# Output weights of six heads per layer by transfers of eight rows, in place of two or three heads by transfers of four

## Chip, cores and metric

The kernel runs on one core of one Trainium2 chip. The metric is the device time of one execution in microseconds (us), the median of several runs. Every microsecond in a profile counts from the start of the profiled execution's span.

## The reference

Two layers are computed, with the same weights and the same key and value cache in both. Each is a grouped-query attention block for decoding (two sequences, one new token each) followed by a gated feed-forward block, with residual additions.

```python
def _A_ref(x, k_cache, v_cache, wq, wo):          # x [2, 1, 512], caches [2, 8, 32768, 128]
    q = (x @ wq).reshape(B, Sq, Hq, Dh).transpose(0, 2, 1, 3)   # 32 query heads of 128
    k = jnp.repeat(k_cache, rep, axis=1)                         # 4 query heads per cached head
    v = jnp.repeat(v_cache, rep, axis=1)
    scores = jnp.einsum("bhqd,bhkd->bhqk", q, k) * (Dh ** -0.5)
    p = _softmax(scores, axis=-1)
    o = jnp.einsum("bhqk,bhkd->bhqd", p, v)
    return o.transpose(0, 2, 1, 3).reshape(B, Sq, Hq * Dh) @ wo

def _B_ref(x, w_gate, w_up, w_down):              # 512 -> 1792 -> 512
    h = _gelu(x @ w_gate) * (x @ w_up)
    return h @ w_down

x = x + _A_ref(_layernorm(x), ...)
x = x + _B_ref(_layernorm(x), ...)
x = x + _A_ref(_layernorm(x), ...)
x = x + _B_ref(_layernorm(x), ...)
```

All values are 32-bit floats. The caches alone are 537 MB, and each layer reads nearly all of them.

## The kernel before

The kernel keeps one large tile `mem` of 128 partitions by 109 units; a unit is 512 floats per partition. All weights and cache pieces pass through it. `stream` is a queue, written out in advance, of every transfer in the order in which its data are used. `pump` (L183) takes transfers from its head for as long as the next one fits into a hole of `mem`, and issues them on the SyncE queue (SP). `get` hands a landed piece to TensorE and `done` gives its units back and pumps again. So the depth of the queue in front of the DMA engines is set by how early units come free. Most cache pieces are 32 units (`CHUNK`), and three of them and 13 spare units fill `mem`. Pieces that are cut fine at the layer boundary have places written out by hand in `plan`.

Within a layer the loop runs over 16 pairs of cached head and sequence (`orders`; layer 1 goes backwards). For each pair, `scores` multiplies the query by the keys (L414), `softmax` follows, `values` multiplies by the values (L485), and `combine` leaves the four query heads' outputs in `oT`. After both sequences of a cached head, `project` multiplies `oT` by the head's slices of the output weights and adds into the PSUM bank `W`. The output weights come in groups of one or two cached heads (`WO_GROUPS`), queued between the two halves of a value transfer. The last cached head of a layer goes by `last_head` (L559). Then follow `residual` and `feedforward` (gate and up weights in four pieces for each of two halves, L638; down weights, L623 and L559).

For one cached head per layer, listed in `NARROW`, some of the query heads' weights don't lie on all 128 partitions. They are laid out on 16 (`NROW`) partitions, so that each row is eight times as long. In layer 0 this is head 6 with two of its four query heads, in layer 1 head 1 with three. Their transfer is issued as four transfers of four rows each:

```python
for i in range(4):
    nc.sync.dma_start(mem[i:NROW:4, c:c + cols], src[i])
```

Row r of such a transfer lies on partition i + 4r. `narrow` cuts `oT` into eight slices of 16 rows by matmuls with columns of the identity (L511), copies them to SBUF (L514), and multiplies each slice by its part of the weights (L519). The remaining query heads of that cached head come by an ordinary transfer of 128 partitions and are multiplied at L529. Narrow weights always take a whole `CHUNK` of 32 units.

Of the kernel before, what the change touches and what calls it, by code (L numbers as in the profile page):

```python
# [16 lines left out]
P = 128  # L17
NB = 2
HKV = 8
REP = 4  # L20
DM = 512
# [6 lines left out]
HALF = 2048  # L28
# [11 lines left out]
ORDER = [(g, b) for g in range(HKV) for b in range(NB)]  # L40
# [19 lines left out]
WO_GROUPS = [[(0, 1), (2, 3), (4, 5), (6,), (7,)], [(7,), (6,), (5, 4), (3, 2), (1,), (0,)]]  # L60


NARROW = {(0, HKV - 2): 2, (1, 1): 3}
NROW = 16
NSEL = P // NROW


def pieces(split):

    out, s = [], 0  # L70
    for n in split:
        out.append((s, n))
        s += n
    return out
# [61 lines left out]
def block_kernel(ctx: ExitStack, tc: tile.TileContext, x, consts, kt, vt, wq, wo, won, gu, wd, out):  # L136
    nc = tc.nc
# [12 lines left out]
    def take(key, n):  # L150
        if key in planned:
            o = planned[key]
            if not any(s <= o and o + n <= e for s, e in holes):
                return None
        elif n == CHUNK:
            spots = [o for o in range(0, UNITS - CHUNK + 1, CHUNK)
                     if any(s <= o and o + n <= e for s, e in holes)]
            if not spots:
                return None
            o = spots[0]  # L160
        else:
            fit = [(e - s, -s, e) for s, e in holes if e - s >= n]
            if not fit:
                return None
            size, s, e = min(fit)
            o = -s
        for i, (s, e) in enumerate(holes):
            if s <= o and o + n <= e:
                holes[i:i + 1] = [(x, y) for x, y in ((s, o), (o + n, e)) if y > x]
                return o  # L170
        return None

    def give(o, n):
        holes.append((o, o + n))
        holes.sort()
        i = 0
        while i + 1 < len(holes):
            if holes[i][1] == holes[i + 1][0]:
                holes[i:i + 2] = [(holes[i][0], holes[i + 1][1])]
            else:  # L180
                i += 1

    def pump():  # L183
        while stream:
            key, src, rows, cols = stream[0]
            n = CHUNK if rows == NROW else cols / UNIT if key in planned else -(-cols // UNIT)
            o = take(key, n)
            if o is None:
                return
            stream.popleft()  # L190
            c = int(o * UNIT)
            at[key] = (o, n), mem[:rows, c:c + cols]
            if rows == NROW:


                for i in range(4):
                    nc.sync.dma_start(mem[i:NROW:4, c:c + cols], src[i])
            else:
                nc.sync.dma_start(at[key][1], src)

    def flat_of(key):
        if key not in at:
            pump()
        return at[key][1]

    def get(key, a):
        return flat_of(key).rearrange("p (a c) -> p a c", a=int(a))

    def done(key, s=0, n=None):
# [10 lines left out]
    def flat(src, g, b, s, n):  # L220
        h, c = divmod(s, CHUNK)
        return src[b, g, h, :, c * UNIT:(c + n) * UNIT]

    def add(key, src, rows, cols):
        stream.append((key, src, rows, cols))

    def meets(l, n):

        return (l == 0 and n == len(ORDER) - 1), (l == 1 and n == 0)

    def wo_group(l, g):
        return next(t for t in WO_GROUPS[l] if g in t)

    for l in range(2):
        for i, (s, m) in enumerate(pieces(WQ_SPLIT[l])):
            add(("wq", l, i), wq[:, s * DM:(s + m) * DM], P, m * DM)
        for n, (g, b) in enumerate(orders[l]):
            second = meets(l, n)[1]
            vp = parts("v", l, (g, b))
            for s, m in parts("k", l, (g, b)):  # L240
                add(("k", l, g, b, s), flat(kt, g, b, s, m), P, m * UNIT)
            for s, m in [] if second else vp:
                if n % 2 == 1 and s == vp[1][0] and not meets(l, n)[0]:
                    group = wo_group(l, g)
                    o = g % 2 * HALF
                    if (l, g) in NARROW:
                        h = NARROW[l, g]
                        add(("won", l, g), won[l, :, :, :h * NSEL * DM], NROW, h * NSEL * DM)
                        add(("wo", l, g), wo[g // 2, :, o + h * DM:o + HALF], P, (REP - h) * DM)
                    elif len(group) == 2 and g == group[0]:  # L250
                        add(("wo", l, g), wo[g // 2], P, 2 * HALF)
                    elif len(group) == 1:
                        add(("wo", l, g), wo[g // 2, :, o:o + HALF], P, HALF)
                add(("v", l, g, b, s), flat(vt, g, b, s, m), P, m * UNIT)
            if meets(l, n)[0]:

                add(("wo", l, g), wo[g // 2, :, g % 2 * HALF:(g % 2 + 1) * HALF], P, HALF)
        for e in range(2):
            half_of = gu[e * P * FH:(e + 1) * P * FH].rearrange("(p c) -> p c", p=P)
            for j, (c, m) in enumerate(pieces(GU_SPLIT[l])):  # L260
                add(("gu", l, len(GU_SPLIT[l]) * e + j), half_of[:, c:c + m], P, m)
        for j, (o, m) in enumerate(pieces(WD_SPLIT[l])):
            add(("wd", l, j), wd[:, o * DM:(o + m) * DM], P, m * DM)
# [5 lines left out]
    def cut(n=1, shape=None):  # L269
# [12 lines left out]
    ident = cst[:, C_ID:C_ID + P]  # L282
# [22 lines left out]
    twice = {n: [cut(m, k) for _ in range(2)] for n, m, k in  # L305
             [("rstd", 1, None), ("ls", 2, None), ("xn", KC * NB, KC), ("oT", REP * NB, REP)]}
# [4 lines left out]
    def tiny(name):  # L311
        if name in once:
            return once[name]
        twice[name].reverse()
        return twice[name][1]
# [4 lines left out]
    W = ps.tile([P, 512], F32, name="W")  # L320
# [181 lines left out]
        diag = bass.AP(tensor=mt.tensor, offset=mt.offset, ap=[mt.ap[0], [1, REP], [P + REP, 4], [32, 4]])  # L502
        nc.vector.tensor_reduce(oT[:, :, b], diag, axis=AX.XY, op=OP.add)  # L503

    def narrow(l, g, oT, final):

        m = small()
        heads = NARROW[l, g]
        n = heads * NB
        for j in range(NSEL):  # L510
            nc.tensor.matmul(m[:NROW, n * j:n * j + n], ident[:, NROW * j:NROW * j + NROW],  # L511
                             oT[:, :heads, :].rearrange("p t b -> p (t b)"), start=True, stop=True)
        on = big()[:NROW, :NSEL * n]
        nc.vector.tensor_copy(on, m[:NROW, :NSEL * n])  # L514
        w = get(("won", l, g), NSEL * heads)
        for i in range(NSEL * heads):
            q = i % 4
            j, t = i % NSEL, i // NSEL
            nc.tensor.matmul(W[32 * q:32 * q + NB, :], on[:, n * j + NB * t:n * j + NB * t + NB], w[:, i, :],  # L519
                             start=False, stop=(final and q < heads and i + 4 >= NSEL * heads))  # L520
        done(("won", l, g))

    def project(l, g, oT, first, final):
        if (l, g) in NARROW:
            narrow(l, g, oT, final)
            h = NARROW[l, g]
            w = get(("wo", l, g), REP - h)
            for t in range(h, REP):
                nc.tensor.matmul(W[32 * t:32 * t + NB, :], oT[:, t, :], w[:, t - h, :], start=False, stop=final)  # L529
            done(("wo", l, g))  # L530
            return
        group = wo_group(l, g)
        key = "wo", l, group[0]
        w = get(key, REP * len(group))
        o = REP * (g - min(group))
        for t in range(REP):
            nc.tensor.matmul(W[32 * t:32 * t + NB, :], oT[:, t, :], w[:, o + t, :], start=first, stop=final)  # L537
        if g == group[-1]:
            done(key)

# [126 lines left out]
    for l in range(2):  # L667
        queries(l)
        stage(l, 0)
        for n, (g, b) in enumerate(orders[l]):  # L670
            if n % 2 == 0:
                oT = tiny("oT")
            p, linv = softmax(*scores(l, n, g, b))
            if meets(l, n)[0]:
                stash(g, b)
            stage(l, n + 1)
            values(l, n, g, b, p)
            combine(linv, oT, b, 128 if n == len(ORDER) - 1 else 0)
            if n == len(ORDER) - 1:
                last_head(l, g, oT)  # L680
            elif n % 2 == 1:
                project(l, g, oT, n == 1, n == len(ORDER) - 3)
            if n == len(ORDER) - 3:
                turn(xin)
        residual()
        feedforward(l)
        if l == 0:
            residual()
# [58 lines left out]
```

## Time and profile before

| | before |
|---|---|
| time, median of 3 runs | 2570.76 us (2570.63 to 2570.87) |
| span of the profiled execution | 2568.7 us |
| TensorE busy | 1374.8 us (54%) |
| VectorE, ScalarE, GpSimd busy | 143.6, 81.4, 2.4 us |
| moved by the SP queue | 1103.44 MB in 27136 packets |
| mean rate over the span | 430 GB/s |

The profile is of one execution; its span runs from the first to the last profiled instruction, and the measured time lies 2.1 us above it. The page lists busy time by engine, then the span in 40 slices, the DMA queues, the chain of work that ended last (each step followed back to what released it), the costliest groups of instructions, and the DMA issues. Queues are told by number: q1 is what SP issues, q8 carries instructions to the engines. A transfer of 128 partitions is spread over the 16 DMA engines, eight rows to each; the trace gives a packet's time and size but not its engine. In the window view a row has, after the engines' busy times, the granted TensorE clock, the mean busy share of the 16 DMA engines and the GB/s that they moved. In the view of transfers for a window, "under 512 B" counts packets by size, each class including the smaller ones.

### The profile page before, as it was taken

The page shows a single profiled execution, that of the slowest core. Times are in us where ns is not written, and L with a number is a line of the kernel's source. Part 1 is how long each engine was busy: PE and PEld are TensorE (multiplying, and loading weights), DVE is VectorE, ACT ScalarE, POOL GpSimd, SP SyncE. Part 2 cuts the span into 40 slices and gives each one's busy share as a digit, 9 for nine tenths or more (in the row PEclk, how much of TensorE's full clock was granted, in tenths as well). Part 3 has the DMA queues.
Part 4 walks back from the last instruction along what each step waited for, and adds up shares of the span by engine and source line. Part 5 has one row for each costly group of instructions (what it writes and reads, how often), then busy time and mean ns, then how long its engine had stood idle before and what let it go on. Part 6 is the DMA issues. An engine that isn't in the chain of part 4 may idle for free.

```text
span 2568.7 us, 20340 instructions
## 1 busy us (share of the span) xinstructions
PE 1374.8 (54%) x9526; PEld 369.8 (14%) x9526; DVE 143.6 (6%) x483; ACT 81.4 (3%) x188; POOL 2.4 (0%) x8
## 2 busy tenths in 40 slices
PE   3545555545544554564686554454555544554657
PEld 1111111111111111111121111111111111111112
DVE  0000000000000000000011000000000000000001
ACT  0000000000000000000000000000000000000000
POOL 0000000000000000000000000000000000000000
PEclk8777777777777777777798677677776777777779
DMA  9999999999999999999999999999999999999998
GB/s 425 429 434 434 428 437 431 432 433 434 429 438 428 435 433 431 434 431 432 424 410 438 429 433 434 430 433 435 431 434 432 431 435 431 433 433 430 431 432 371
DMA packets 27507, 1104.81 MB, mean 430 GB/s; under 512 B 3200, under 2 KB 3456, under 8 KB 6912
## 3 DMA queue, kind: packets, MB, share of 16 engines
q1 hardware_dynamic: 27136, 1103.44, 99.6%
q8 instruction: 74, 1.21, 0.2%
q10 hardware_dynamic: 288, 0.08, 0.0%
q14 instruction: 9, 0.07, 0.0%
HBM read 1103.45 MB, written 0.07 MB: 430 GB/s over the span
## 4 chain that ended last, share of the span: by engine, by line
DMA 69%; PE 22%; another core or an unknown queue 8%; DVE 1%; issue 0%; ACT 0%; SPq 0%; POOL 0%; ACTq 0%; DVEq 0%
DMA mem<-in_vt 41%; DMA mem<-in_kt 24%; PE A L485 11%; PE S L414 9%; DMA aux<-in_consts 2%; DMA mem<-in_gu 1%; DMA mem<-in_wq 1%; DMA mem<-in_wd 0%; PE W L537 0%; PE M L498 0%; ACT big L494 0%; PE T L460 0%; PE W L519 0%; PE W L559 0%
## 5 line engine op out<-in xcount | busy, mean ns | idle before, releaser
L414 PE MATMUL S<-mem,aux 128*32 128x512 f32 x4032 | 575.5, 734 | 527.1 <-DMA mem<-in_kt 526.7
L485 PE MATMUL A<-mem,big 128*16 128x512 f32 x4096 | 584.7, 734 | 480.8 <-DMA mem<-in_vt 480.8
L414 PEld LDWEIGHTS S<-mem,aux 128*32 128x32 f32 x4032 | 144.9, 132 | 945.3 <-issue 508.2
L485 PEld LDWEIGHTS A<-mem,big 128*16 128x16 f32 x4096 | 122.6, 113 | 913.5 <-DMA mem<-in_vt 514.9
L417 DVE TENSOR_REDUCE aux<-S 128x1 f32<-128x512 f32 x63 | 43.6, 691 | 1110.1 <-PE S L414 1110.1
L457 ACT ACTIVATE big<-S,aux 128x512 f32<-128x512 f32 x63 | 42.7, 683 | 1187.1 <-DVE aux L453 1187.1
L460 PE MATMUL T<-aux,big 128*128 128x128 f32 x256 | 50.2, 342 | 39.0 <-ACT big L457 38.7
L503 DVE TENSOR_REDUCE aux<-M 128x4 f32<-128x64 f32 x32 | 7.2, 225 | 1103.4 <-PE M L498 1103.4
L494 ACT ACTIVATE big<-A,aux 128x512 f32<-128x512 f32 (+1 forms) x34 | 22.3, 661 | 1149.0 <-PE A L485 1149.0
L461 DVE COPY big<-T 128x512 f32<-128x512 f32 x64 | 43.8, 691 | 59.8 <-PE T L460 59.8
L460 PEld LDWEIGHTS T<-aux,big 128*128 128x128 f32 x256 | 35.8, 172 | 49.7 <-ACT big L457 49.5
L498 PE MATMUL M<-aux,big 128*128 128x128 f32 x128 | 21.3, 287 | 24.9 <-ACT big L494 24.9
L465 PE MATMUL M<-aux 128*128 128x4 f32 x64 | 17.2, 339 | 29.4 <-DVE aux L463 29.4
L449 PE MATMUL M<-aux 128*128 128x128 f32 x32 | 10.3, 323 | 34.5 <-DVE aux L447 34.5
L373 PE MATMUL M<-mem,aux 128*32 128x512 f32 x128 | 20.6, 690 | 4.4 <-DMA mem<-in_wq 3.9
L498 PEld LDWEIGHTS M<-aux,big 128*128 128x128 f32 x128 | 13.4, 140 | 53.2 <-ACT big L494 53.2
L465 PEld LDWEIGHTS M<-aux 128*128 128x128 f32 x64 | 14.4, 280 | 39.1 <-DVE aux L463 39.1
L537 PE MATMUL W<-mem,aux 128*2 128x512 f32 x96 | 12.5, 592 | 3.8 <-DVE aux L503 3.8
L333 PE MATMUL A<-aux 128*128 128x256 f32 (+2 forms) x42 | 14.3, 421 | 0.3 <-DVE aux L350 0.3
L449 PEld LDWEIGHTS M<-aux 128*128 128x128 f32 x32 | 4.2, 133 | 63.6 <-DVE aux L447 63.6
L359 PE MATMUL M<-aux 128*128 128x8 f32 x2 | 0.6, 356 | 23.2 <-DMA aux<-in_x 23.2
L457 ACT ACTIVATION_READ_ACCUMULATOR big<-S,aux 128x1 f32 x63 | 12.3, 196 | 0.0
(102 smaller groups left out, 188.8 us busy)
## 6 DMA issues: line engine op xcount, KB each, us to landing
mem<-in_gu SPq DMA_DIRECT2D x16, 896.0 KB, 24.5
mem<-in_wo SPq DMA_DIRECT2D x5, 2048.0 KB, 53.5
mem<-in_vt SPq DMA_DIRECT2D x2, 4096.0 KB, 42.2
mem<-in_kt SPq DMA_DIRECT2D x1, 7168.0 KB
mem<-in_wq SPq DMA_DIRECT2D x6, 1024.0 KB, 8.2
mem<-in_kt SPq DMA_DIRECT2D x1, 6144.0 KB
mem<-in_kt SPq DMA_DIRECT2D x5, 1024.0 KB, 8.7
mem<-in_kt SPq DMA_DIRECT2D x1, 4352.0 KB
```

Of the source, the lines that this page charges most:

```text
L333: nc.tensor.matmul(bank, ident[:, :bank.shape[0]], part.to_broadcast([P, n]), start=True, stop=True)
L373: nc.tensor.matmul(qp[32 * t:32 * t + 32, :], window(k, v), w[:, i - s, :], start=(i < 4), stop=(i >= 8 * KC - 4))
L414: nc.tensor.matmul(banks[u][32 * t:32 * t + 32, :], pad[:, PAD_Q - 4 * c:PAD_Q + 32 - 4 * c], w[:, j - s, :], start=(j == tile_of[0]), sto ...
L417: nc.vector.tensor_reduce(mx[:, u:u + 1], banks[u], axis=AX.X, op=OP.max)
L449: nc.tensor.transpose(m[:, :P], nm.to_broadcast([P, P]), ident)
L457: nc.scalar.activation(p[u], banks[u], AF.Exp, bias=bias, scale=SCALE, accum_out=ls[:, u:u + 1])
L460: nc.tensor.transpose(T[u][:, k * P:(k + 1) * P], p[u][:, k * P:(k + 1) * P], ident)
L461: nc.vector.tensor_copy(p[u], T[u])
L465: nc.tensor.matmul(m[:, :REP], both.to_broadcast([P, P]), same, start=True, stop=True)
L485: nc.tensor.matmul(A[32 * t:32 * t + 16, :], p[u][:, at_p:at_p + 16], w[:, QUAD * i + t, :], start=(j == 0), stop=(j == NU // QUAD - 1))
L494: nc.scalar.activation(md[:, i:i + 512 // n], A[:, i:i + 512 // n], AF.Copy, scale=linv)
L498: nc.tensor.transpose(m[:, c * P:(c + 1) * P], md[:, c * P:(c + 1) * P], ident)
```

## The change

Six query heads per layer, not two or three, get the narrow layout: all four of the cached head in `NARROW`, and two of the cached head before it in the order of work (5 in layer 0, 2 in layer 1). They lie on 32 partitions, in four slices instead of eight, and each of the four transfers has eight rows of 49,152 bytes on partitions i, i + 4, ..., i + 28. The narrow head's ordinary transfer goes, and that of the group before it is cut to six heads (`wide`; `apart` lists the heads that are left out). `narrow` takes the outputs of the two heads of the cached head before from the other `oT` buffer.

```diff
-NARROW = {(0, HKV - 2): 2, (1, 1): 3}
-NROW = 16
+NARROW = {(0, HKV - 2): [(HKV - 3, 2), (HKV - 3, 3)], (1, 1): [(2, 0), (2, 1)]}
+NARROW = {(l, g): more + [(g, t) for t in range(REP)] for (l, g), more in NARROW.items()}
+NROW = 32
 NSEL = P // NROW
+NHEADS = 2 + REP
...
+    def apart(l, g):
+        return [t for heads in (NARROW[k] for k in NARROW if k[0] == l) for h, t in heads if h == g]
+
+    def wide(l, group):
+        own = [REP * (g - min(group)) + t for g in group for t in range(REP) if t not in apart(l, g)]
+        return min(own), max(own) + 1
...
                     if (l, g) in NARROW:
-                        h = NARROW[l, g]
-                        add(("won", l, g), won[l, :, :, :h * NSEL * DM], NROW, h * NSEL * DM)
-                        add(("wo", l, g), wo[g // 2, :, o + h * DM:o + HALF], P, (REP - h) * DM)
+                        add(("won", l, g), won[l], NROW, NHEADS * NSEL * DM)
                     elif len(group) == 2 and g == group[0]:
-                        add(("wo", l, g), wo[g // 2], P, 2 * HALF)
+                        a, e = wide(l, group)
+                        add(("wo", l, g), wo[g // 2, :, a * DM:e * DM], P, (e - a) * DM)
...
-    def narrow(l, g, oT, final):
+    def narrow(l, g, oT, before, final):
         m = small()
         heads = NARROW[l, g]
-        n = heads * NB
+        n = NHEADS * NB
+        k = n - REP * NB
+        first = heads[0][1]
         for j in range(NSEL):
-            nc.tensor.matmul(m[:NROW, n * j:n * j + n], ident[:, NROW * j:NROW * j + NROW],
-                             oT[:, :heads, :].rearrange("p t b -> p (t b)"), start=True, stop=True)
+            row = ident[:, NROW * j:NROW * j + NROW]
+            nc.tensor.matmul(m[:NROW, n * j:n * j + k], row,
+                             before[:, first:first + NHEADS - REP, :].rearrange("p t b -> p (t b)"), start=True, stop=True)
+            nc.tensor.matmul(m[:NROW, n * j + k:n * j + n], row,
+                             oT.rearrange("p t b -> p (t b)"), start=True, stop=True)
         on = big()[:NROW, :NSEL * n]
         nc.vector.tensor_copy(on, m[:NROW, :NSEL * n])
-        w = get(("won", l, g), NSEL * heads)
-        for i in range(NSEL * heads):
+        w = get(("won", l, g), NSEL * NHEADS)
+        for i in range(NSEL * NHEADS):
             q = i % 4
-            j, t = i % NSEL, i // NSEL
+            t, j = divmod(i, NSEL)
...
         if (l, g) in NARROW:
-            narrow(l, g, oT, final)
-            h = NARROW[l, g]
-            w = get(("wo", l, g), REP - h)
-            for t in range(h, REP):
-                nc.tensor.matmul(W[32 * t:32 * t + NB, :], oT[:, t, :], w[:, t - h, :], start=False, stop=final)
-            done(("wo", l, g))
+            narrow(l, g, oT, before, final)
             return
...
         for t in range(REP):
-            nc.tensor.matmul(W[32 * t:32 * t + NB, :], oT[:, t, :], w[:, o + t, :], start=first, stop=final)
+            if t not in apart(l, g):
+                nc.tensor.matmul(W[32 * t:32 * t + NB, :], oT[:, t, :], w[:, o + t, :], start=first, stop=final)
...
-                oT = tiny("oT")
+                oT, before = tiny("oT"), twice["oT"][0]
```

On the host the array `won` is arranged anew to match.

More of the change, by code (lines that the diff above doesn't have):

```diff
@@ L503, in combine, with project @@
         nc.vector.tensor_reduce(oT[:, :, b], diag, axis=AX.XY, op=OP.add)
-    def narrow(l, g, oT, final):
+    def narrow(l, g, oT, before, final):
         m = small()
         heads = NARROW[l, g]
-        n = heads * NB
+        n = NHEADS * NB
+        k = n - REP * NB
+        first = heads[0][1]
         for j in range(NSEL):
-            nc.tensor.matmul(m[:NROW, n * j:n * j + n], ident[:, NROW * j:NROW * j + NROW],
-                             oT[:, :heads, :].rearrange("p t b -> p (t b)"), start=True, stop=True)
+            row = ident[:, NROW * j:NROW * j + NROW]
[3 more added lines that the diff above has]
+                             oT.rearrange("p t b -> p (t b)"), start=True, stop=True)
         on = big()[:NROW, :NSEL * n]
         nc.vector.tensor_copy(on, m[:NROW, :NSEL * n])
-        w = get(("won", l, g), NSEL * heads)
-        for i in range(NSEL * heads):
+        w = get(("won", l, g), NSEL * NHEADS)
+        for i in range(NSEL * NHEADS):
             q = i % 4
-            j, t = i % NSEL, i // NSEL
+            t, j = divmod(i, NSEL)
             nc.tensor.matmul(W[32 * q:32 * q + NB, :], on[:, n * j + NB * t:n * j + NB * t + NB], w[:, i, :],
-                             start=False, stop=(final and q < heads and i + 4 >= NSEL * heads))
+                             start=False, stop=(final and i + 4 >= NSEL * NHEADS))
         done(("won", l, g))
-    def project(l, g, oT, first, final):
+    def project(l, g, oT, before, first, final):
         if (l, g) in NARROW:
-            narrow(l, g, oT, final)
-            h = NARROW[l, g]
-            w = get(("wo", l, g), REP - h)
-            for t in range(h, REP):
-                nc.tensor.matmul(W[32 * t:32 * t + NB, :], oT[:, t, :], w[:, t - h, :], start=False, stop=final)
-            done(("wo", l, g))
+            narrow(l, g, oT, before, final)
             return
@@ L533, in project @@
         key = "wo", l, group[0]
-        w = get(key, REP * len(group))
-        o = REP * (g - min(group))
+        a, e = wide(l, group)
+        w = get(key, e - a)
+        o = REP * (g - min(group)) - a
         for t in range(REP):
-            nc.tensor.matmul(W[32 * t:32 * t + NB, :], oT[:, t, :], w[:, o + t, :], start=first, stop=final)
+            if t not in apart(l, g):
+                nc.tensor.matmul(W[32 * t:32 * t + NB, :], oT[:, t, :], w[:, o + t, :], start=first, stop=final)
         if g == group[-1]:
@@ L681, in block_kernel @@
             elif n % 2 == 1:
-                project(l, g, oT, n == 1, n == len(ORDER) - 3)
+                project(l, g, oT, before, n == 1, n == len(ORDER) - 3)
             if n == len(ORDER) - 3:
@@ L730 @@
         "wo": f(np.asarray(A_wo).reshape(HKV // 2, 2 * REP, P, DM).transpose(0, 2, 1, 3)).reshape(HKV // 2, P, 2 * HALF),
-        "won": f(np.asarray(A_wo).reshape(HKV, REP, NSEL, 4, 4, DM)[[g for _, g in NARROW]]
-                 .transpose(0, 4, 3, 1, 2, 5)).reshape(len(NARROW), 4, 4, REP * NSEL * DM),
+        "won": f(np.asarray(A_wo).reshape(HKV * REP, NSEL, NROW // 4, 4, DM)
+                 [[[REP * g + t for g, t in heads] for heads in NARROW.values()]]
+                 .transpose(0, 4, 3, 1, 2, 5)).reshape(len(NARROW), 4, NROW // 4, NHEADS * NSEL * DM),
         "gu": halves(np.asarray(B_w_gate), np.asarray(B_w_up)),
```

## Prediction

> **What bounds the kernel now.** I read the page first: span, busy time by engine, the transfer queues, the chain that ended last. Then the transfer view and the window view, stretch by stretch, around the places where the change acts.
>
> ```profile
> span 2568.7 us, 20340 instructions
> PE 1374.8 (54%) x9526; PEld 369.8 (14%) x9526; DVE 143.6 (6%) x483; ACT 81.4 (3%) x188; POOL 2.4 (0%) x8
> DMA packets 27507, 1104.81 MB, mean 430 GB/s; under 512 B 3200, under 2 KB 3456, under 8 KB 6912
> q1 hardware_dynamic: 27136, 1103.44, 99.6%
> q8 instruction: 74, 1.21, 0.2%
> DMA 69%; PE 22%; another core or an unknown queue 8%; DVE 1%; issue 0%; ACT 0%; SPq 0%; POOL 0%; ACTq 0%; DVEq 0%
> ```
>
> The kernel is a stream of transfers. TensorE works 54% of the span, transfers stand for 69% of the chain, and the stream moves 430 GB/s nearly throughout. The span is 2568.7 us and the median of the runs 2570.76, so about 2.1 us lie outside the span; I add them unchanged.
>
> So the change can matter only where the stream isn't full, or where a transfer's slowest share is waited for. Two window answers show where that is: microseconds 1287 to 1289 (layer 0's attention gives way to its feed-forward part), with two 14 us stretches for scale, and the last ones. The last two columns are the DMA share and GB/s.
>
> ```profile
> 1287.00:1288.00 1.00, 0.91 (x10) 0.55 (x13) 0.30 (x2) 0.17 (x1) 0.00 (x0) 1.00 0.74 308
> 1288.00:1289.00 1.00, 1.00 (x33) 0.75 (x33) 0.00 (x0) 0.00 (x0) 0.00 (x0) 1.00 0.76 315
> 1285.00:1299.00 14.00, 9.80 (x95) 3.99 (x98) 2.10 (x13) 1.81 (x6) 0.55 (x1) 1.00 0.93 370
> 1200.00:1214.00 14.00, 6.73 (x44) 1.53 (x48) 0.00 (x0) 0.00 (x0) 0.00 (x0) 0.63 0.99 431
> ...
> 2557.00:2558.00 1.00, 1.00 (x10) 0.17 (x2) 0.00 (x0) 0.24 (x1) 0.00 (x0) 1.00 0.81 332
> 2558.00:2559.00 1.00, 0.52 (x4) 0.13 (x6) 0.73 (x2) 0.24 (x1) 0.00 (x0) 1.00 0.75 311
> 2559.00:2560.00 1.00, 0.62 (x6) 0.00 (x0) 0.76 (x3) 0.51 (x1) 0.00 (x0) 1.00 0.72 303
> 2560.00:2561.00 1.00, 0.86 (x4) 0.47 (x4) 0.47 (x2) 0.00 (x0) 0.00 (x0) 1.00 0.73 303
> 2561.00:2562.00 1.00, 1.00 (x10) 0.11 (x8) 0.04 (x1) 0.00 (x0) 0.00 (x0) 1.00 0.76 309
> 2562.00:2563.00 1.00, 1.00 (x6) 0.30 (x2) 0.00 (x0) 0.52 (x1) 0.00 (x0) 1.00 0.51 201
> 2563.00:2564.00 1.00, 1.00 (x26) 0.59 (x28) 0.00 (x0) 0.07 (x1) 0.00 (x0) 1.00 0.21 84
> 2564.00:2565.00 1.00, 1.00 (x47) 0.90 (x40) 0.00 (x0) 0.00 (x0) 0.00 (x0) 1.00 0.10 37
> ```
>
> A share of 0.75 means that 12 of 16 DMA engines still work. At both places four engines are done about 5 us before most others. That staircase is what the change can remove. At the end the shares missing from 2557 to 2565 add up to 3.4 us (0.19 + 0.25 + 0.28 + 0.27 + 0.24 + 0.49 + 0.79 + 0.90): if all 16 stopped together, the stream would end 3.4 us earlier. At the boundary 14 us at 370 instead of 431 GB/s lose 2.0 us. The ceiling of any rebalancing is 5.4 us, 0.21%. About 0.2% (5.1 us) is what a measurement of this kernel can tell from no change.
>
> **Why four engines are early.** Each engine closes each transfer with a 4-byte packet, so "under 512 B" in a short window of the transfer view counts engines that have reached that mark. The rows are, in order: 59.8 to 62.2 us; 1081.4 to 1083.6, 1083.6 to 1086.1 and 1086.1 to 1088.1 (just before layer 0's narrow transfer); 1100.8 to 1104.6 and 1104.6 to 1109 (after it); 1256.9 to 1260.5, 1260.5 to 1264 and 1264 to 1265.4 (one mark near the end of layer 0); 2331.4 to 2334.6, 2334.6 to 2337.8 and 2337.8 to 2341 (just before layer 1's).
>
> ```profile
> DMA packets 31, 1.05 MB, mean 437 GB/s; under 512 B 15, under 2 KB 15, under 8 KB 15
> DMA packets 23, 0.98 MB, mean 447 GB/s; under 512 B 8, under 2 KB 8, under 8 KB 8
> DMA packets 16, 1.05 MB, mean 419 GB/s; under 512 B 0, under 2 KB 0, under 8 KB 0
> DMA packets 23, 0.98 MB, mean 492 GB/s; under 512 B 8, under 2 KB 8, under 8 KB 8
> DMA packets 76, 1.41 MB, mean 371 GB/s; under 512 B 19, under 2 KB 19, under 8 KB 51
> DMA packets 154, 2.13 MB, mean 484 GB/s; under 512 B 29, under 2 KB 29, under 8 KB 125
> DMA packets 33, 1.51 MB, mean 419 GB/s; under 512 B 4, under 2 KB 4, under 8 KB 4
> DMA packets 43, 1.38 MB, mean 393 GB/s; under 512 B 10, under 2 KB 10, under 8 KB 10
> DMA packets 19, 0.56 MB, mean 398 GB/s; under 512 B 2, under 2 KB 2, under 8 KB 2
> DMA packets 29, 1.38 MB, mean 430 GB/s; under 512 B 8, under 2 KB 8, under 8 KB 8
> DMA packets 20, 1.31 MB, mean 410 GB/s; under 512 B 0, under 2 KB 0, under 8 KB 0
> DMA packets 30, 1.44 MB, mean 451 GB/s; under 512 B 8, under 2 KB 8, under 8 KB 8
> ```
>
> Early on 15 marks fall within 2.4 us. By 1081 us the sixteen have split into eight and eight, with 2.5 us of nothing between them and about 4.6 us from middle to middle. What fits is queue 8: instruction fetches of 16 KB, 74 in all, if only eight engines serve them (my inference; no view names the engine). After the narrow transfer the 4 KB packets of the transfer behind it (the "under 8 KB" ones that aren't marks) come as 51 - 19 = 32, four engines' eight rows, and then 125 - 29 = 96, twelve engines'. So the four engines that carried the narrow rows came from the early half: extra bytes moved them back among the late eight. The other four early ones stayed ahead, which is the staircase.
>
> **The change part by part.** An engine moves 431 / 16 = 27.0 bytes per ns. A head's weights are 128 x 512 x 4 = 262,144 bytes, 16,384 per engine if spread over 16.
>
> ```profile
> mem<-in_won SPq DMA_DIRECT2D x4, 192.0 KB
> mem<-in_won SPq DMA_DIRECT2D x4, 128.0 KB
> ```
>
> Layer 0, six heads. Before: two heads over four engines (4 x 128 KB, so 131,072 bytes each) and four heads over 16 (65,536 each). After: six heads over eight, 196,608 each, nothing on the rest. The four narrow engines: 131,072 + 65,536 = 196,608, unchanged. The four that join them: +131,072, or +4.85 us. The other eight: -65,536, or -2.43 us.
>
> Layer 1. Before: three heads over four (196,608 each), three over 16 (49,152 each). After the same 196,608 on eight. The first four: -49,152, or -1.82 us. The four joining: +147,456, or +5.46 us. The other eight: -1.82 us.
>
> Who is last, then? In layer 0 the mark at 1257 to 1265 us shows the four early, ten more by 1264 and two stragglers after it, up to 1.2 us behind the ten. Those two must be fetch engines, the only ones that keep being hit. They go forward by 2.43 us; the narrow four among the ten stay. So the last engine moves from the stragglers to the back of the ten: -1.2 us. The bounds are 0 (a narrow engine is last already) and 2.0 (the whole loss). In layer 1 the last engine, whether narrow or late, is relieved of 1.82 us, and the four joining need 5.46 us of the 5 to 8 us by which they are early: -1.8 us. The bounds are 0.8 (the eight that carry the weights start layer 1 up to 1 us later against the others, because less of the lag is worn off at the boundary) and 3.4 (the whole staircase).
>
> Does the last engine set the end at both places? These pieces of the chain say so: the end waits for gate weights, then a fixed tail follows. The same view shows what the end of the narrow projection releases.
>
> ```profile
> 2539.20 17.39 DMA mem<-in_gu
> ...
> 1145.03 41.85 DMA mem<-in_vt
> ```
>
> TensorE: layer 0's narrow projection grows, and two heads beside it go.
>
> ```profile
> L519 PE MATMUL W<-mem,big 16*2 16x512 f32 x32 | 4.3, 677 | 0.3 <-DVE big L514 0.3
> L529 PE MATMUL W<-mem,aux 128*2 128x512 f32 x4 | 1.9, 1036 | 0.0
> L511 PE MATMUL M<-aux 128*16 128x4 f32 x16 | 0.6, 167 | 0.3 <-DVE aux L503 0.3
> L197 SPq DMA_DIRECT2D mem<-in_won x8: 576/577/724, 1075.9 to 2330.1; - x8
> ```
>
> 24 head slices instead of 16 are 4.3 x 24/16 = 6.5 us, the 1.9 us disappear, and the selections stay 16 records at 0.6 us: +0.3 us in layer 0. In layer 1 the slices stay 24 and one wide head goes, so less. I cost it at nothing: the cover is the queued stream, because the transfer released at 1145.03 lands 41.85 us later while its own data take about 19. Without that cover it would cost 0.3 us. On SP the four narrow issues stay at 0.58 us each and one wide issue per narrow stage goes; the narrow rows take the same 32 units of memory as before. No wait is added: the next value transfer on the same engines lands after the narrow one anyway.
>
> The Trainium skill speaks against the shape. "DMA: Bandwidth & Descriptors", Rules for kernel authors, asks for an outermost dimension that is a multiple of 16, since fewer rows confine a transfer to as many engines. The 32 and 96 packets agree on the confinement, but they also show the other engines going on with the next transfer; by the rule alone 1.5 MB at half speed would cost 7.3 us a layer and not 3.6, by the trace it costs only its share.
>
> **Sum.** -1.2 - 1.8 + 0 = -3.0 us: span 2565.7, and with the 2.1 us around it **2567.8 us**, inside the 0.2%.
>
> **The rivals.**
>
> *The four that join are not the early four* (slower). Nothing in this trace ties the early four to the row positions that eight rows add. If those rows go to engines that serve instruction fetches, late engines get +4.85 us in layer 0 and +5.46 in layer 1, on top of being late. Set against the last engine now, about +4.8 at each boundary: 2570.8 + 9.6 = 2580.4. It decides as soon as one of the four is in the late half. Against it: the four narrow engines were all early, 4 of 4, and a block of eight neighbours is the simplest reading of eight and eight. The same skill page, Why a DMA increments its semaphore by 16 and not by 1, says that such a transfer takes the lowest-numbered engines; by that alone nothing follows on who fetches. Chance 0.16.
>
> *The whole staircase goes* (faster). If the engines end together at both places, 5.4 us go: 2565.4. For it: +4.85 and +5.46 us are close to the lead of the four. Against it: fetches keep hitting single engines after the narrow transfer, and the last windows show single stragglers (0.21, 0.10) that no even shift removes. Chance 0.10.
>
> *No gain.* The last share is set by something that doesn't move: 2570.8. The 2.43 us taken off the late eight speak against it. Chance 0.11.
>
> **How the numbers follow.** Forecast 0.63. Faster by over 0.2% is the second rival, 0.10; slower the first, 0.16; within 0.2% the forecast and no gain, 0.74. The range goes from 2565.3 (the whole staircase) to 2570.9 (no gain) and leaves out the slow rival.
>
> **What would show it.** Right: the last microseconds hold near 1.0 until about 2562 and then fall at once; at 1287 to 1289 the share stays above 0.9; the mark after layer 0's narrow transfer comes as one group. Wrong: a share of 0.75 or less that lasts 8 us or more at those places, which means that late engines got the rows, or the same staircase as now.

## The result, and the profile after

| | before | after |
|---|---|---|
| time, median of 5 runs each | 2570.67 us (2570.59 to 2570.87) | 2578.91 us (2578.8 to 2579.05) |
| span of the profiled execution | 2568.7 us | 2577.0 us |

The change makes the kernel slower by 8.2 us: a ratio of 1.0032, interval [1.002, 1.0044]. It is the first rival of the prediction that came about.

From the page of the kernel after, its first rows and its queues, and from its view of transfers the row of the narrow ones:

```profile
span 2577.0 us, 20342 instructions
PE 1377.4 (53%) x9528; PEld 371.5 (14%) x9528; DVE 143.7 (6%) x483; ACT 81.4 (3%) x188; POOL 2.4 (0%) x8
DMA packets 27283, 1104.81 MB, mean 429 GB/s; under 512 B 3200, under 2 KB 3456, under 8 KB 6656
q8 instruction: 74, 1.21, 0.2%
mem<-in_won SPq DMA_DIRECT2D x8, 384.0 KB
```

The bytes are the same to the last digit shown, the narrow rows come in eight issues of 384 KB, TensorE has 2.6 us more of work, and the stream moves 429 GB/s on the mean instead of 430. So the same stream takes longer. The chain of work that ended last, in order of time, tells where. Two pieces of the kernel after, the last value piece of layer 0 and the last gate weights (start, length, what):

```profile
1264.51 25.39 DMA mem<-in_vt
...
2547.42 17.37 DMA mem<-in_gu
```

Before, the piece that answers to the first was this:

```profile
1262.31 22.86 DMA mem<-in_vt
```

Layer 0's last values land at 1289.90 us instead of 1285.17, 4.7 us later. The last gate weights land at 2564.79 instead of 2556.59, 8.2 us later, and what follows them takes as long as before. So 4.7 us are lost by the layer boundary, and 3.5 more by the end. Both places look alike in the window view. First the boundary, with 16 us around it; then the last microseconds before the stream ends; and last a stretch after layer 1's narrow transfer (last two columns: DMA share and GB/s):

```profile
1290.00:1291.00 1.00, 1.00 (x9) 0.15 (x9) 0.00 (x0) 0.00 (x0) 0.00 (x0) 1.00 0.51 211
1291.00:1292.00 1.00, 0.82 (x5) 0.47 (x5) 0.00 (x0) 0.84 (x2) 0.00 (x0) 1.00 0.18 74
1292.00:1293.00 1.00, 0.91 (x17) 0.71 (x20) 0.30 (x2) 0.00 (x0) 0.00 (x0) 1.00 0.17 72
1293.00:1294.00 1.00, 1.00 (x30) 0.75 (x22) 0.00 (x0) 0.14 (x1) 0.00 (x0) 1.00 0.14 57
1285.00:1301.00 16.00, 12.91 (x110) 4.72 (x110) 1.13 (x10) 1.21 (x4) 0.55 (x1) 1.00 0.75 276
...
2566.00:2567.00 1.00, 0.51 (x5) 0.13 (x6) 0.53 (x2) 0.44 (x1) 0.00 (x0) 1.00 0.71 287
2567.00:2568.00 1.00, 0.84 (x6) 0.00 (x0) 0.76 (x3) 0.51 (x1) 0.00 (x0) 1.00 0.43 168
2568.00:2569.00 1.00, 0.66 (x3) 0.47 (x4) 0.47 (x2) 0.00 (x0) 0.00 (x0) 1.00 0.12 49
2569.00:2570.00 1.00, 1.00 (x6) 0.11 (x8) 0.24 (x1) 0.00 (x0) 0.00 (x0) 1.00 0.14 57
2570.00:2571.00 1.00, 1.00 (x9) 0.30 (x2) 0.00 (x0) 0.32 (x1) 0.00 (x0) 1.00 0.11 45
2571.00:2572.00 1.00, 1.00 (x18) 0.38 (x20) 0.00 (x0) 0.28 (x1) 0.00 (x0) 1.00 0.14 57
2572.00:2573.00 1.00, 1.00 (x45) 0.91 (x40) 0.00 (x0) 0.00 (x0) 0.00 (x0) 1.00 0.10 37
...
2335.00:2404.00 69.00, 33.79 (x231) 8.93 (x235) 3.46 (x13) 2.13 (x5) 0.00 (x0) 0.69 0.99 423
```

A share of 0.12 is two engines of sixteen. Where the kernel before had a step at 0.75, twelve engines working and four done, now fourteen are done and two work on alone for 3 to 5 us (0.10 to 0.18). At the boundary 16 us at 276 instead of 431 GB/s lose 16 x 155 / 431 = 5.8 us, where the kernel before lost 2.0. The last stretch loses less, some 1.1 us: its 423 GB/s stand against 430 in a stretch of about the same length of the kernel before:

```profile
2330.00:2400.00 70.00, 38.12 (x267) 9.75 (x271) 4.09 (x14) 2.13 (x5) 0.00 (x0) 0.73 1.00 430
```

How two engines fell back shows in the marks, counted in the view of transfers by windows as in the prediction. The kernel after, in order: 1080.1 to 1082.6, 1082.6 to 1085.3 and 1085.3 to 1086.9 us (just before layer 0's narrow transfer); 1119.1 to 1119.4, 1119.4 to 1124, 1124 to 1128.6, 1128.6 to 1132.5 and 1132.5 to 1132.8 (after it).

```profile
DMA packets 26, 1.18 MB, mean 472 GB/s; under 512 B 8, under 2 KB 8, under 8 KB 8
DMA packets 17, 1.11 MB, mean 413 GB/s; under 512 B 0, under 2 KB 0, under 8 KB 0
DMA packets 21, 0.85 MB, mean 532 GB/s; under 512 B 8, under 2 KB 8, under 8 KB 8
...
DMA packets 7, 0.33 MB, mean 1092 GB/s; under 512 B 2, under 2 KB 2, under 8 KB 2
DMA packets 27, 1.77 MB, mean 385 GB/s; under 512 B 0, under 2 KB 0, under 8 KB 0
DMA packets 43, 2.03 MB, mean 442 GB/s; under 512 B 12, under 2 KB 12, under 8 KB 12
DMA packets 24, 1.57 MB, mean 403 GB/s; under 512 B 0, under 2 KB 0, under 8 KB 0
DMA packets 6, 0.26 MB, mean 874 GB/s; under 512 B 2, under 2 KB 2, under 8 KB 2
```

Before the narrow transfer there are eight and eight, as in the kernel before. After it there are two, twelve and two. If all eight narrow rows had gone to early engines there would be one group. Two, twelve and two is what comes out if six went to early engines and two to late ones: two early engines without rows stay ahead, six early with rows meet six late without, and two late with rows trail by 13.4 us. That is a reading of counts; no view names an engine. The experiments test it.

### The profile page after: what moved, and what is told of

Same layout as the page of the kernel before. It is cut to its first block, busy times and chain, and to the rows that moved or that the text cites. A ratio compares the mean times of both kernels' runs of the same rounds, so it can differ in the third digit from the quotient of the medians.

```text
span 2577.0 us, 20342 instructions
## 1 busy us (share of the span) xinstructions
PE 1377.4 (53%) x9528; PEld 371.5 (14%) x9528; DVE 143.7 (6%) x483; ACT 81.4 (3%) x188; POOL 2.4 (0%) x8
## 4 chain that ended last, share of the span: by engine, by line
DMA 69%; PE 22%; another core or an unknown queue 7%; DVE 1%; ACT 0%; issue 0%; SPq 0%; POOL 0%; ACTq 0%; DVEq 0%
DMA mem<-in_vt 45%; DMA mem<-in_kt 21%; PE A L495 12%; PE S L424 8%; DMA aux<-in_consts 2%; DMA mem<-in_gu 1%; DMA mem<-in_wq 1%; PE W L534 0%; DMA mem<-in_wd 0%; PE W L549 0%; PE M L508 0%; ACT big L504 0%; DVE big L471 0%; PE W L571 0%
## 5 line engine op out<-in xcount | busy, mean ns | idle before, releaser
L475 PE MATMUL M<-aux 128*128 128x4 f32 x64 | 16.6, 329 | 29.4 <-DVE aux L473 29.4
L459 PE MATMUL M<-aux 128*128 128x128 f32 x32 | 10.3, 323 | 34.6 <-DVE aux L457 34.6
L508 PEld LDWEIGHTS M<-aux,big 128*128 128x128 f32 x128 | 13.4, 141 | 53.2 <-ACT big L504 53.2
L534 PE MATMUL W<-mem,big 32*2 32x512 f32 x96 | 18.9, 962 | 0.6 <-DVE big L529 0.6
```

Source lines behind the costliest of these rows:

```text
L459: nc.tensor.transpose(m[:, :P], nm.to_broadcast([P, P]), ident)
L475: nc.tensor.matmul(m[:, :REP], both.to_broadcast([P, P]), same, start=True, stop=True)
L508: nc.tensor.transpose(m[:, c * P:(c + 1) * P], md[:, c * P:(c + 1) * P], ident)
```

## The experiments

The theory, A, is this: the row positions of a narrow transfer are served by engines in a fixed order, the fifth to eighth of which are not all early; two are engines that instruction fetches slow down. Extra bytes on them set the end of each layer. The rivals put the time on the six heads' work on TensorE, on the 32 partitions, or on the size of the change instead of on who gets the rows, and one of them doubts that the fetches make half of the engines late. All comparisons are against the kernel before unless the text says otherwise.

### A ruler: which engines are early

The kernel before, with markers on another queue: after pair n of layer 0 (n from 3 to 15) a transfer of n + 1 rows of 12 bytes.

```diff
+    mark = cut(3)
...
+            if l == 0 and n >= 3:
+                nc.scalar.dma_start(mark[:n + 1], consts[:n + 1, :3])
```

> The kernel before, with 13 extra tiny transfers in layer 0 on ScalarE's queue: 12 bytes per row, with 4 rows after the fourth pair, 5 rows after the fifth, and so on to 16 rows after the last. In the trace each 12-byte packet follows a packet of one of the sixteen engines, so each further row names one more engine as early or late. Theory A (of the eight engines that eight-row transfers use, two serve instruction fetches): the 4-row transfer falls on four early engines, the 8-row one on six early and two late, the 16-row one on eight and eight. Rival B (eight rows fall on the eight early engines, and the loss has another cause, the longer narrow projection on TensorE or its wait): the 8-row transfer falls on eight early engines. Time: within 1 us of before under both.

The one run took 2571.35 us, within the 1 us that was expected, so the ruler hardly disturbs the stream. Its 130 rows are seen twice each in ScalarE's queue (548 packets instead of 288):

```profile
q10 hardware_dynamic: 548, 0.08, 0.0%
```

In the records of single packets I followed each 12-byte packet through the packets that begin where the last one ends, to the 4-byte mark that closes the value or key transfer its engine is in. How far behind the first mark of the group these lie, in us (a lag of 19 to 20 us is one piece of 19.4 us further on, and is counted by the group in which it falls there; with 12 and 13 rows one of the early lags by 2.2 us, where the first late one lags by more than 4):

| rows | early, lag of its last | late, lag |
|---|---|---|
| 4 | 4, 1.0 | none |
| 5 | 5, 1.0 | none |
| 6 | 5, 1.1 | 1, 3.1 |
| 7 | 5, 1.1 | 2, 3.0 to 3.1 |
| 8 | 6, 1.2 | 2, 3.1 to 3.2 |
| 9 | 7, 1.2 | 2, 4.6 to 4.7 |
| 10 to 13 | 7 | 3, 4, 5, 6 |

Each further row adds one engine to those before it. Counted from zero, the row positions 0 to 4, 7 and 8 are early, and 5, 6 and 9 to 12 are late. Those from 13 on fall behind the narrow transfer and can't be read. So four rows lie on four early engines, as the prediction found, and eight rows on six early and two late. The Trainium skill, "DMA: Bandwidth & Descriptors", Why a DMA increments its semaphore by 16 and not by 1, ties the number of engines to the number of rows; the ruler agrees from 4 to 13 rows, and adds which of them are late, on which the page has nothing for this kernel.

### Eight rows with the few heads of before

```diff
-NROW = 16
+NROW = 32
```

Two heads in layer 0 and three in layer 1, as before, but 32 partitions and four transfers of eight rows (the host array is arranged to match).

> The same two and three heads on 32 partitions, by four transfers of eight rows, so eight DMA engines share them. Theory A: the two late engines among the eight get 65,536 bytes more than before in layer 0 and 98,304 in layer 1, 2.4 and 3.6 us at 27 bytes per ns, and they were last already: 6.1 us slower, about 2576.8. Rival B: fewer heads, so the projection on TensorE is as long as before: 2570 to 2571, or faster, since the bytes are spread more evenly.

Measured: 2574.84 us (2574.38 to 2575.47), ratio 1.0015 [1.0006, 1.0025], so +4.0 us. Neither number was met. A rival that needs the six heads would give no loss here, and a loss of nothing lies outside the interval, so eight rows alone cost time. The end of the stream in the window view of this kernel:

```profile
2563.00:2564.00 1.00, 0.51 (x7) 0.05 (x1) 0.66 (x2) 0.44 (x1) 0.00 (x0) 1.00 0.57 236
2565.00:2566.00 1.00, 1.00 (x9) 0.11 (x8) 0.00 (x0) 0.00 (x0) 0.00 (x0) 1.00 0.38 152
2567.00:2568.00 1.00, 1.00 (x33) 0.74 (x36) 0.00 (x0) 0.00 (x0) 0.00 (x0) 1.00 0.13 53
```

The step goes down slowly, 0.57, 0.38, 0.13: the two late engines have less extra load and trail less. Why A was 2 us too high is worked out below.

### Four rows on 32 partitions

```diff
-NROW = 16
+NROW = 32
...
-                for i in range(4):
-                    nc.sync.dma_start(mem[i:NROW:4, c:c + cols], src[i])
+                for i in range(8):
+                    nc.sync.dma_start(mem[i:NROW:8, c:c + cols], src[i])
```

> The kernel before (two heads in layer 0, three in layer 1), but on 32 partitions, by eight transfers of four rows each (rows i, i + 8, i + 16, i + 24), so that the same four DMA engines carry the same bytes as before. Theory A: as before, 2570.7 us within 0.5. A cause that lies in the 32 partitions, or in multiplying slices of 32 rows: slower by a part of the 8.2 us, 1 us or more.

Measured: 2582.13 us (2581.72 to 2583.58), ratio 1.0046 [1.0029, 1.0062], +11.3 us where A expected none. A missed, but for a reason outside the question. SyncE's own waits around layer 0's narrow transfer (line waited for: total, times, longest):

```profile
SPq L197 <- DMA mem<-in_vt: 20.8, 1, 20.8
SPq L197 <- DMA mem<-in_kt: 12.1, 1, 12.1
```

L197 is the issue of the narrow transfers. It is issued eight times instead of four, and SyncE held back the seventh and the eighth until transfers issued long before had landed. In the records of landings this program, like the kernel before, counts all its landings on eight semaphores. With four issues more in a row, each of these came round sooner, SyncE waited for the one it needed, and the queue in front of the engines ran dry: from 1100 to 1130 us they moved 317 GB/s. In layer 1 the same two issues waited 10.6 and 20.0 us. The run says nothing on 32 partitions. It shows another price: narrow transfers in this kernel can't be cut into more pieces.

### A third of the new projection

The kernel after, with 8 of the 24 weight slices of a layer multiplied, and all of them transferred.

```diff
-        for i in range(NSEL * NHEADS):
+        for i in range(8):
...
-                             start=False, stop=(final and i + 4 >= NSEL * NHEADS))
+                             start=False, stop=(final and i + 4 >= 8))
```

> The changed kernel, whose narrow projection multiplies 8 of its 24 slices only (the other sixteen are left out of the result); all transfers are the changed kernel's. Theory A: as changed, 2578.9 within 0.5. Rival B (TensorE's longer projection): most of the 8.2 us return, 2571 to 2574.

Measured: 2578.92 us (2578.7 to 2579.14), ratio 1.0031 [1.0019, 1.0043]. The groups of the narrow multiply, the kernel after and then this one:

```profile
L534 PE MATMUL W<-mem,big 32*2 32x512 f32 x96 | 18.9, 962 | 0.6 <-DVE big L529 0.6
```

```profile
L534 PE MATMUL W<-mem,big x32: 586/792/1056, 1144.6 to 2405.2; 32*2 32x512 f32 x32
```

64 of 96 records are gone and the time is that of the kernel after (2578.91). The projection's work on TensorE isn't the cost.

### One layer at a time

Layer 0 as after and layer 1 as before (an entry has the query heads, the partitions and the rows of a transfer; the code that reads it is left out here):

```diff
-NARROW = {(0, HKV - 2): 2, (1, 1): 3}
+NARROW = {(0, 6): ([(5, 2), (5, 3), (6, 0), (6, 1), (6, 2), (6, 3)], 32, 8), (1, 1): ([(1, 0), (1, 1), (1, 2)], 16, 4)}
```

> The change in layer 0 alone, layer 1 as before. Theory A: the late two of the eight engines lose at the boundary; 3 to 4.8 us of the 8.2, 2574 to 2575.5, and after it the end is as before. Rival (one layer carries all of it): 2570.8 or 2578.9.

Measured: 2575.08 us (2573.87 to 2575.82), ratio 1.0016 [1.0007, 1.0026], +4.3 us. The window view shows the late pair at the boundary and the old end:

```profile
1292.00:1293.00 1.00, 0.91 (x17) 0.71 (x20) 0.30 (x2) 0.00 (x0) 0.00 (x0) 1.00 0.14 57
...
2567.00:2568.00 1.00, 1.00 (x6) 0.30 (x2) 0.00 (x0) 0.60 (x1) 0.00 (x0) 1.00 0.56 219
```

Layer 1 as after and layer 0 as before:

```diff
-NARROW = {(0, HKV - 2): 2, (1, 1): 3}
+NARROW = {(0, 6): ([(6, 0), (6, 1)], 16, 4), (1, 1): ([(2, 0), (2, 1), (1, 0), (1, 1), (1, 2), (1, 3)], 32, 8)}
```

> The change in layer 1 alone. Theory A: the rest of the 8.2 us, 3.5 to 5.3 us, 2574 to 2576; with the run for layer 0 alone the two losses add up to 8.2 within 1 us.

Measured: 2574.87 us (2573.79 to 2576.45), ratio 1.0016 [1.0007, 1.0025], +4.1 us, and the mirror image in the windows:

```profile
1287.00:1288.00 1.00, 0.82 (x6) 0.57 (x6) 0.00 (x0) 0.58 (x2) 0.00 (x0) 1.00 0.78 324
...
2564.00:2565.00 1.00, 1.00 (x6) 0.11 (x8) 0.27 (x1) 0.00 (x0) 0.00 (x0) 1.00 0.12 49
```

4.3 + 4.1 = 8.4 us, against 8.2 for both: two losses that add up, one at the end of each layer. Single executions of these two kernels lie up to 2.7 us apart, so the halves are less sure than their sum.

### Five rows and six

If the sixth engine is the first late one, five rows are free of late engines and six are not. Three heads per layer on 20 or 24 partitions, in four transfers of five or six rows, and a fifth transfer of four rows for the last eight of the 128 rows of each head, which don't divide. In the cut shown, `rows` is 20 or 24 and `step` is 4.

```diff
+                for i in range(step):
+                    nc.sync.dma_start(mem[i:rows:step, c:c + wide_of], main[i])
+                nc.sync.dma_start(mem[:4, c + wide_of:c + cols], last)
```

Five rows:

> Three heads in each layer on 20 partitions, by four transfers of five rows (the last eight rows of each head by one transfer of four rows); the rest as before. By the ruler the first five engines are early. Theory A: they get 1.94 us per head ahead of the rest moved back, 5.8 us a layer, which the late eight then don't trail: 2569.3 us, between 2568.5 and 2570.7. Rival C (the more partitions and rows, the slower): slower than before, 2571.5 or more.

Measured: 2570.89 us (2570.54 to 2575.16), ratio 1.0002 [0.9993, 1.0011]. Just outside what was expected, and no gain. The end of its stream in the window view:

```profile
2559.00:2560.00 1.00, 0.71 (x6) 0.00 (x0) 0.75 (x3) 0.51 (x1) 0.00 (x0) 1.00 0.81 340
2562.00:2563.00 1.00, 1.00 (x10) 0.30 (x2) 0.00 (x0) 0.43 (x1) 0.00 (x0) 1.00 0.49 193
2564.00:2565.00 1.00, 1.00 (x44) 0.86 (x40) 0.00 (x0) 0.00 (x0) 0.00 (x0) 1.00 0.07 29
```

0.81 is thirteen engines: three are early now and not four, so the fifth was an early one. But the stream's last engines end at the same time as before, and that is what counts. The gain of 1.4 us that was expected left out what the late engines carried before: by the arrangement they get 16,384 bytes less in layer 0 (0.6 us by the rate) and as many as before in layer 1.

Six rows:

> The same three heads on 24 partitions, by four transfers of six rows. By the ruler the sixth engine is late. Theory A: that one engine gets 122,880 bytes of narrow rows in place of its 49,152, +2.7 us, where the last engine before was relieved by 1.2 and 1.8 us: 4 us at each boundary, together 2577, between 2575 and 2579. Rival C: hardly another time than with five rows, within 1 us.

Measured: 2577.39 us (2577.16 to 2579.3), ratio 1.0028 [1.0016, 1.0039]. The sixth row costs 6.5 us. The time is in the range, but by luck: before, the late engine had 16,384 bytes of these heads in layer 0 and none in layer 1, not 49,152, and to the 2.7 us from that were added reliefs of 1.2 and 1.8 us that the run of the change itself hadn't shown. By the bytes the sum is 8.5 us, and 2 us less was measured (see the table below). What bears on the theory is the step from five rows to six. Its windows at the end:

```profile
2568.00:2569.00 1.00, 1.00 (x4) 0.24 (x2) 0.43 (x1) 0.00 (x0) 0.00 (x0) 0.50 0.16 64
2569.00:2570.00 1.00, 1.00 (x4) 0.58 (x3) 0.42 (x1) 0.00 (x0) 0.00 (x0) 0.71 0.06 25
2572.00:2573.00 1.00, 1.00 (x26) 0.57 (x28) 0.00 (x0) 0.08 (x1) 0.00 (x0) 1.00 0.06 25
```

0.06 is one engine of sixteen. It works on alone for some 4 us, where the kernel with eight rows has two (0.12). One late engine among six rows, two among eight: as the ruler counted. This is the pair of runs that decides for A.

### More instruction fetches

That late engines are late because they serve the fetches was inferred. The kernel before with 1,920 tiny multiplies added into a place that nobody reads, to lengthen the instruction stream; the transfers of the stream are the same:

```diff
+                    if not first and not second:
+                        nc.tensor.matmul(T[1][:NB, 511:512], ident[:, :NB], part, start=True, stop=True)
```

> The kernel before with 1,920 extra tiny matmuls (2 x 1 results that nothing reads) between the value matmuls of 30 pairs: about 7,700 more TensorE records, so about 30 more 16 KB fetches on queue 8 (74 now for 19,052 records). No transfer of the stream changes. Theory A (fetches make eight engines late): the late eight trail the early eight at 1081 us by about 1.4 times as much as before (6.5 in place of 4.6 us), and each boundary comes 2 to 3.5 us later: 2575 to 2578 us. Rival D (the eight are late for another cause, fetches only happen to be there): the gap at 1081 us stays at 4.6 us, and the time within 1 us of 2570.8.

Measured: 2575.97 us (2575.23 to 2577.74), ratio 1.002 [1.0011, 1.003], +5.2 us. Its page has 28020 instructions instead of 20340, and

```profile
q8 instruction: 104, 1.70, 0.3%
```

30 fetches more for 7,680 instructions more is 256 to a fetch. The marks at 1081.2 to 1083.9, 1083.9 to 1089.2 and 1089.2 to 1091.4 us:

```profile
DMA packets 27, 1.25 MB, mean 461 GB/s; under 512 B 8, under 2 KB 8, under 8 KB 8
DMA packets 36, 2.36 MB, mean 445 GB/s; under 512 B 0, under 2 KB 0, under 8 KB 0
DMA packets 22, 0.92 MB, mean 417 GB/s; under 512 B 8, under 2 KB 8, under 8 KB 8
```

Still eight and eight, but with 5.3 us of nothing between them instead of 2.5, and 7.8 us from middle to middle instead of 4.6. From the mean of the first eight marks to the mean of the last eight, in the records of single packets, it is 7.8 us instead of 5.1. By 1081 us queue 8 had carried, in the kernel before and then in this one:

```profile
q8 instruction: 29, 0.48, 0.2%
q8 instruction: 42, 0.69, 0.3%
```

1.45 times the fetches go with 1.5 times the lag. The same records show that a fetch takes 1.07 us on its engine and that the data packet behind it takes 0.5 us longer than others, 1.56 us in all on the mean. Shared by eight engines that is an estimate of 29 x 1.56 / 8 = 5.7 us and 42 x 1.56 / 8 = 8.2 us, 2.5 us apart where 2.6 are measured. So the fetches account for the lag, in both kernels.

What the lag costs is shown for layer 0 only. Three pieces of this kernel's chain, and TensorE's row of its page:

```profile
1266.54 21.91 DMA mem<-in_vt
...
2474.55 48.05 DMA mem<-in_vt
2522.64 1.92 PE A L485 x5
...
PE 1505.1 (58%) x13366; PEld 465.2 (18%) x13366; DVE 143.9 (6%) x483; ACT 81.5 (3%) x188; POOL 2.4 (0%) x8
```

Layer 0's last values land at 1288.45 us, 3.3 us later than before, as was expected of a boundary, and up to 1270 us the DMA share stays at 0.99 or more in windows of 60 to 130 us, so the stream hardly paused before that. But the extra multiplies also give TensorE 130.3 us more of work. From 2522.6 us on the chain has no landing any more, only the engines' own work, where the kernel before waited for gate weights until 2556.59. So the end of this run isn't set by the stream alone, the time fell into its range partly for another reason, and how much of the 5.2 us is the fetches' can't be told. The Trainium skill, "Runtime: NRT & Kernel Launch", Instruction fetch mechanics, tells of blocks of 16 KiB with 256 instructions each and calls the cost of crossing into the next one mostly hidden. The size and the count agree. The 1.56 us that each fetch takes from an engine that moves data are not hidden from a stream that fills these engines.

## Why the prediction was wrong

**The step that failed** is the one under "the four that join": that the engines of row positions 4 to 7 are the four early ones that the narrow rows of before leave free. The trace of before proved four, and the step from there was "a block of eight neighbours is the simplest reading". It isn't so: positions 4 and 7 are early, 5 and 6 late, and position 8, outside the block, is early too. So two of the joining four needed their bytes while already behind. A guess about a layout that no row showed carried a chance of 0.63, and the rival with the right mechanism got 0.16 and was left out of the range.

**The terms of the sum** fall with it. -1.2 us in layer 0 and -1.8 in layer 1 were reliefs of the last engine. The other six late engines were relieved, but positions 5 and 6 took their place as the last: +4.7 and +3.5 us by the chain, +4.3 and +4.1 by the two runs with one layer each.

**The rival's price** was 4.8 + 4.8 = 9.6 us, against 8.2. Bytes added to a late engine, by 27.0 bytes per ns (estimated from the arrangement and the rate), against what was measured:

| kernel | added in layer 0 and layer 1 | by the rate | measured |
|---|---|---|---|
| layer 0 only | 131,072 and 0 | 4.9 us | 4.3 us |
| layer 1 only | 0 and 147,456 | 5.5 us | 4.1 us |
| after | 131,072 and 147,456 | 10.3 us | 8.2 us |
| eight rows, few heads | 65,536 and 98,304 | 6.1 us | 4.0 us |
| six rows | 106,496 and 122,880 | 8.5 us | 6.6 us |

0.6 us are missing in layer 0 and 1.4 in layer 1; together that is the 1.9 to 2.1 us missing in the last three rows. What fits is that the late engines that got the rows weren't the last ones before, and had that much to spare, as the mark at the end of layer 0 hinted (two stragglers up to 1.2 us behind the others). This also is the 2 us by which the expectation for eight rows was too high. That there is such slack is worked out from the five numbers, not seen in a row of its own.

**What held.** Half of the engines lag by instruction fetches (their count accounts for the lag in two kernels), and who gets the narrow rows decides who ends last. TensorE was rightly costed at nothing, though its size was off: the narrow multiplies and the wide ones beside them took 12.0 + 3.7 = 15.7 us before and the narrow ones alone 18.9 us after, 3.2 us more, where layer 0 was to cost 0.3 us and layer 1 less. The run with a third of the slices shows that none of it counts. The rival with its price of 9.6 us had its condition right: one late engine among the rows is enough, as the run with six rows shows. The windows that the prediction named as a sign against it, a share of 0.75 or less for 8 us or more, turned up deeper and shorter: down to 0.10 within 7 us at the end, and to 0.14 within 6 us at the boundary. The ceiling of rebalancing, 5.4 us, wasn't reached by any kernel here.

**What stays open.** Which of the positions 13 to 15 is the eighth early one. How much of the 5.2 us of the run with more fetches is theirs. And what a longer wait costs: from 1118 to 1165 us, behind layer 0's narrow transfer, SyncE waits longer for a landing before it may issue again,

```profile
SPq L201 <- DMA mem<-in_vt: 16.3, 1, 16.3
```

where it was 11.1 us at the same place before (in layer 1, 16.6 us against 11.5). Whether this is what layer 1's stretch at 423 GB/s loses, some 1.1 us, wasn't measured.

## What to carry to other kernels

A transfer of fewer than sixteen rows loads some engines only (seen here for 4 to 13 rows), so find out first which are early: a handful of tiny marker transfers with one row more each, in a kernel that runs as before, reads the order off for nothing. Four of four early isn't eight of eight, and a count of how many engines lag says nothing on where they are in the order. Where a stream ends with its slowest engine, taking bytes off the others buys nothing, and one late engine with more bytes costs nearly the whole of them (6.6 us of 8.5 with six rows). An experiment that adds instructions also adds work: look at what its chain ends on before its time is put down to the stream.

## What the runs showed of the hardware

Instruction fetches ride on the engines that move data. 74 fetches of 16 KB over 2570 us are 0.2% of the engines' time, but by the counts of marks they go to eight of the sixteen only, so half of the engines fall behind: by 4.6 us up to 1081 us with 29 fetches until then, by 7.8 us with 42. The eight aren't neighbours: of the row positions that could be read, 5, 6 and 9 to 12 are among them, and 0 to 4, 7 and 8 are not. In the packets' records the engine that serves a fetch of 16 KB is held up by about 1.56 us, where 64 KB of data take 2.42 us: 1.07 us for the fetch, and 0.5 us more for the data packet behind it.

And the transfers under way are limited by their count as well as by memory: with eight landing semaphores in turn, cutting the narrow weights of a layer into eight issues in place of four made SyncE wait 12.1 and 20.8 us in layer 0, and the kernel took 11.3 us longer.
